# Another order for the first groups: chunks 4 and 5 ahead of weights, scores ahead of state products, q of the first chunks scaled by VectorE

## The chip, the cores and the metric

The kernel runs on one NeuronCore of a Trainium2 chip. A core has five instruction queues that run at the same time and wait for each other by semaphores: TensorE (PE in the profile; its weight loads are PEld), VectorE (DVE), ScalarE (ACT), GpSimd (POOL) and SyncE (SP, which here only issues DMA transfers). Each of them takes its instructions strictly in the order in which the program wrote them. Time is device microseconds (us) from start to end of an execution; lower is better.

## The reference

Two stages. The first is linear attention with a decay per head, over 4 batches, 8 heads, 768 positions and 64 features per head, in blocks of 64 positions. The second takes the result as 3072 tokens of 512 features through a two-layer network with a leaky ReLU.

```
for b in range(nb):                       # blocks of 64 positions
    intra = einsum('bhic,bhjc->bhij', qb, kb) * Dmask
    intra = einsum('bhij,bhjd->bhid', intra, vb)
    inter = einsum('bhid,bhde->bhie', qb * lam_pow, kv_state)
    out[:, :, sl] = intra + inter
    kv_state = lam_block * kv_state + einsum('bhsd,bhse->bhde', kb * rev_pow, vb)
x = out.transpose(0, 2, 1, 3).reshape(3072, 512)
h = x @ w_in                              # 512 x 2048, float64 input
return maximum(0.01 * h, h) @ w_out       # 2048 x 512, float64 input
```

## The kernel before, in words

**Tiling.** The tokens are cut into 24 chunks of 128 (two blocks of 64 each; 6 chunks per batch), and chunks are gathered into 6 groups of 4 (`GC = 4`, 512 tokens). The hidden width of 2048 is cut into 8 weights of 256 columns (`NP`), called p. Both products of the network are computed in split form: each operand is held as a high part h, a low part l and a mixed part m (`xh`, `xl`, `xm` for the tokens, `wh`, `wl`, `wm` for weights), and a product is three matmul passes, h by h, l by l and m by m.

**A chunk of attention** goes through these steps.
- `load_kq`, `load_v` (L335, L374): SP issues the loads of k, q (two transfers of 128 KB each) and v (one of 256 KB). The tiles exist twice, by the chunk's parity.
- `transposes` (L389): TensorE turns k and q round. k goes to the PSUM bank named by `KT` (b11) for the first four chunks and to `po` later, q goes to `pt`. ScalarE copies both out (L400, L401).
- L405 scales k in place by a decay, on GpSimd, or for chunks below `KM` on GpSimd or VectorE, whichever the planner sees free first. L409 scales q: for chunks below `QS` VectorE does it straight from `pt`, for others GpSimd from the copy.
- `scores` (L310, writes `psc`): 64 small matmuls in two halves. `go` makes the scores, `kv` makes the state products. Then VectorE masks the scores (L435) and adds the state products to the state (L440 or L442), once for each of the two blocks; between them GpSimd decays the state (L445). `psc` exists once, so the scores of a chunk wait for the last state add of the chunk before.
- `outputs` (L310, writes `po`): `own` and the two halves of `inter`. Then ScalarE makes `xh` (L490), VectorE `xl` (L491) and `xm` (L493; its rank is raised by `LATER` in the first group).

**A weight of w_in** (`w_in`, `to_float32`, `parts`): ScalarE issues two loads of 512 KB (L549); the float64 words are turned into float32 by three ScalarE operations (L561, L563, L565) and two of VectorE (L567, L568) for each half; then come `wh` (L574 on ScalarE or L576 on VectorE), `wl` (L579) and `wm` (L585) on VectorE.

**An up product** `("up", g, p, lo, hi)`: group g by weight p, over chunks lo to hi of the group (all four when they are not given). It is two blocks of 128 hidden columns, each three products of four matmuls (L623) with 512 columns when it is whole; ScalarE scales between the passes (L641) and applies the leaky ReLU (L644); SP writes the result G to DRAM (L647). The result tile `gs` exists twice. The blocks go through banks b10, b11 and b2 in turn; the first `EARLY` blocks leave b11 out.

**Order.** Nothing of this order is found at run time. `seq` lists the steps: `("a", c)` a whole chunk, `("b", c)` loads and transposes of chunks c and c+1 and the scores of c, `("r", c)` a round (outputs of c, scores of c+1, loads and transposes of c+2), `("wi", p)` a weight, `("up", ...)`. A step's place in `seq` is the rank of its operations. `Plan.emit` then schedules all operations in a model of the five queues: it always takes the operation that can start earliest, and among equal ones that of lower rank. The model has a duration for each operation and a delay after it (`LAG`, 3.5 us for a DMA). In the first two groups (the part of `seq` that is written out by hand) a load is taken at its length; later it has a slack of 4 us. While the plan sees TensorE idle early on, it inserts filler transposes into b10 (`busy`, L263), until the first operation that needs b10.

Of the kernel before, what the change touches and what calls it, by code (L numbers as in the profile page):

```python
# [31 lines left out]
def _bc(ap, idx, n):  # L32
    a = [list(x) for x in ap.ap]
    return bass.AP(ap.tensor, ap.offset, a[:idx] + [[0, n]] + a[idx:])


class Plan:
# [23 lines left out]
    def add(self, eng, us, fn, reads=(), writes=(), rank=0.0):  # L61

        n, deps = len(self.ops), set()
        for k in reads:
            w, r = self.last.setdefault(k, [None, []])
            if w is not None:
                deps.add(w)
            r.append(n)
        for k in writes:
            w, r = self.last.setdefault(k, [None, []])  # L70
            if w is not None:
                deps.add(w)
            deps.update(r)
            self.last[k] = [n, []]
        deps.discard(n)
        ways = {eng: us} if isinstance(eng, str) else dict(zip(eng, us))
        if self.slack:
            self.more[n] = self.slack
        if self.chain is not None:
            self.chains[self.chain].append(n)  # L80
        self.ops.append((ways, fn, deps, (self.rank + rank, n), set(writes)))
# [81 lines left out]
def kernel(  # L163
# [21 lines left out]
    NG = NCH // GC  # L185
    T = GC * C
    WARM = 9
    LATER = 4.0
    KT, EARLY = "b11", 1
    QS = 0  # L190
    KM = 1
    NRAW = 3
    TURN = 3
    SLACK, GSLACK = 4.0, 2.0
    SUBL, FIRST = 0.75, -8.0

    DV = 12
# [12 lines left out]
    def ps(shape, name):  # L210
        return psum.tile(shape, F32, name=name, tag=name)
# [3 lines left out]
    psc = ps([P, 2, 2 * HP, C2], "psc")  # L215
# [51 lines left out]
    plan = Plan()  # L267
    plan.idle, plan.spare, plan.warm = busy, "b10", 1.3 + 0.22 * WARM
    add = plan.add
    steady = False  # L270

    def length(us, issue=0.5):

        return issue if steady else us

    def move(us, fn, reads, writes, issue=0.5, rank=0.0, slack=SLACK):

        plan.slack = slack if steady else 0.0
        if steady and not rank:
            rank = FIRST  # L280
        add("DMA", length(us, issue), fn, reads, writes, rank=rank)
        plan.slack = 0.0
# [26 lines left out]
    def quad(dst, rows, lhsT, rhs, cols, start=False):  # L309
        nc.tensor.matmul(dst[HALF[cols]], lhsT=lhsT[HALF[rows]], rhs=rhs[HALF[rows]], start=start, stop=True,  # L310
                         skip_group_check=True)

    def tokens(t):
        return slice(t * C2, (t + 1) * C2)
# [8 lines left out]
    def of(c):  # L323
        return c // NCB, c % NCB, c % 2
# [3 lines left out]
    def load_kq(c):  # L328
        b, n, i = of(c)
        for src, x, nm in ((k, 0, "k"), (q, 1, "q")):  # L330
            y, dst = src[b, :, n * C:(n + 1) * C, :], kqv[x][i]

            def go(y=y, dst=dst):
                for z in range(2):
                    nc.sync.dma_start(out=dst[:, z * HP:(z + 1) * HP, :], in_=y[z::2].rearrange("h p d -> p h d"))  # L335
            if nm == "k" or c < DV:
                move(1.15, go, [], [f"{nm}{i}"], issue=1.0)
# [13 lines left out]
    def load_subs(c):  # L351
        b, n, i = of(c)
        for nm, src, pieces in zip("kq", (k, q), subs(c)):
            for sub, lo, hi, keys in pieces:
                add("DVE", 0.0, lambda: None, [], keys)
                for y in range(lo, hi):
                    for a in range(4):
                        h = y // 2 + (2 * y + a // 2) % HP * 2
                        z = src[b, h, n * C:(n + TURN) * C, a % 2 * C4:(a % 2 + 1) * C4]
                        o = sub[a * C4:(a + 1) * C4, y - lo, :]  # L360
                        move(0.55, lambda o=o, z=z: nc.sync.dma_start(
                                out=o.rearrange("j (m i) -> j m i", i=C4), in_=z.rearrange("(m j) i -> j m i", j=C4)),
                            keys, [f"{nm}s{y}{a}"], issue=SUBL, rank=4.0 + (0.4 if steady else 0.2) * (4 * y + a))
# [8 lines left out]
    def load_v(c):  # L372
        b, n, i = of(c)
        move(1.15, lambda: nc.sync.dma_start(out=kqv[2][i], in_=v[b, :, n * C:(n + 1) * C, :].rearrange("h p d -> p h d")),  # L374
            [], [f"v{i}"])

    def transposes(c):
# [17 lines left out]
        def copies():  # L395
# [3 lines left out]
            if c < DV:  # L399
# [3 lines left out]
            nr = slice(0, C2 if n == NCB - 1 else P)  # L403
            add(*((("DVE", "POOL"), (0.7, 1.1)) if c < KM else ("POOL", 1.1)),
                lambda e="POOL": ENG[e].tensor_tensor(kr[nr], kr[nr], _bc(pow_k, 3, D)[nr], op=ALU.mult), ["fk"], [f"k{i}"])  # L405
            m = slice(1 if n == 0 else 0, 2)
            o, x = (z.rearrange("p y (t i) -> p y t i", t=2)[:, :, m, :] for z in (qsTs[i], pt if c < QS else qTs[i]))
            eng, e, us, dep = ("DVE", nc.vector, 0.7, "pt") if c < QS else ("POOL", nc.gpsimd, 1.2, f"qT{i}")
            add(eng, us, lambda: e.tensor_tensor(o, x, _bc(pow_q, 2, 2)[:, :, m, :], op=ALU.mult), ["fq", dep], [f"qsT{i}"])  # L409
# [3 lines left out]
    def scores(c):  # L413
        b, n, i = of(c)
        tk, tv, kT, qT = kqv[0][i], kqv[2][i], kTs[i], qTs[i]
        n_pu = 1 if n == NCB - 1 else 2

        def go():
            for y in range(HP):
                for t in range(2):  # L420
                    for x in range(2):
                        quad(psc[:, x, y, :], x, kT[:, y, tokens(t)], qT[:, y, tokens(t)], t, start=y == 0)

        def kv():
            for y in range(HP):
                for x in range(2):
                    for t in range(n_pu):
                        h = y // 2 + (2 * y + x) % HP * 2
                        quad(pu[t][:, y, :], t, tk[:, 2 * y + x, :], tv[:, h, :], x, start=y == 0)

        add("PE", 0.47, kv, [f"k{i}", f"v{i}"], ["psc"])
        add("PE", 0.47, go, [f"kT{i}", f"qT{i}"], ["psc"])

        def uses():
            add("DVE", 0.69, lambda: nc.vector.tensor_tensor(sc, psc[:, :, lower, :], decay, op=ALU.mult), ["psc", "fk"], ["sc"])  # L435
            for t in range(n_pu):
                j = 2 * c + t
                new = state[j % 4]
                if n == 0 and t == 0:
                    add("DVE", 0.42, lambda new=new: nc.vector.tensor_copy(new, pu[0]), ["psc"], [f"st{j % 4}"])  # L440
                else:
                    add("DVE", 0.42, lambda new=new, t=t: nc.vector.tensor_tensor(new, new, pu[t], op=ALU.add),  # L442
                        ["psc"], [f"st{j % 4}"])
                if n_pu == 2:
                    add("POOL", 0.7, lambda new=new, j=j: nc.gpsimd.tensor_tensor(state[(j + 1) % 4], new, _bc(lam_c, 2, D), op=ALU.mult),  # L445
                        [f"st{j % 4}", "fq"], [f"st{(j + 1) % 4}"])

        return uses

    def outputs(c, between=lambda: None):  # L450
# [38 lines left out]
        def uses():  # L489
# [3 lines left out]
            add("DVE", 0.7, lambda: nc.vector.scalar_tensor_tensor(xm, xl.bitcast(F32), -S, xh.bitcast(F32), op0=ALU.mult, op1=ALU.add),  # L493
                [h, l], [m], rank=LATER if c < GC else 0.0)

        return uses

    def alone(c):
        load_kq(c)
        load_v(c)  # L500
        transposes(c)()
        scores(c)()
        outputs(c)()

    def begun(c):

        for x in (c, c + 1):
            load_kq(x)
            load_v(x)
            transposes(x)()  # L510
        scores(c)()
# [158 lines left out]
    def down(g, p):  # L670

        nonlocal n_t
        for tb in range(GC):
# [43 lines left out]

    seq = [("a", 0), ("a", 1), ("a", 2), ("a", 3), ("wi", 1), ("b", 4), ("wi", 0), ("up", 0, 1), ("up", 0, 0), ("wi", 2),  # L720
           ("r", 4), ("wi", 3), ("up", 0, 2), ("up", 0, 3), ("r", 5), ("r", 6), ("r", 7), ("wi", 7), ("up", 1, 3, 0, 1),
           ("wi", 4), ("up", 1, 1, 0, 2), ("wi", 6), ("up", 0, 7), ("up", 0, 4), ("up", 1, 7, 1, 3), ("up", 0, 6),
           ("wi", 5), ("up", 0, 5), ("up", 1, 5), ("r", 8), ("r", 9), ("r", 10), ("up", 1, 7, 3, 4), ("r", 11),
           ("up", 1, 2), ("up", 1, 0), ("up", 1, 7, 0, 1), ("up", 1, 3, 1, 4), ("up", 1, 1, 2, 4), ("up", 1, 6),
           ("up", 1, 4)]
    nxt, n_out, begin = 3 * GC, 0, len(seq)
    steps = [(g, p) for g in range(2, NG) for p in range(NP)]
    for n, (g, p) in enumerate(steps):
# [17 lines left out]
    for n, x in enumerate(seq):  # L746
        plan.rank = float(n)
        steady = begin <= n and x[0] in ("r", "up", "wo")
# [50 lines left out]
```

## Time and profile before

| what | value |
|---|---|
| median of 3 runs | 617.78 us (616.84 to 617.81) |
| profiled execution | 617.28 us |
| its span (first to last instruction) | 615.4 us |
| PE busy | 604.8 us, 98% |
| DVE busy | 306.9 us, 50% |
| ACT busy | 270.7 us, 44% |
| POOL busy | 90.6 us, 15% |
| DMA moved | 104.67 MB, 170 GB/s |
| first up product (L623) starts at | 30.67 us |
| chunk outputs (first L310 to `po`) start at | 10.61, 15.02, 21.98, 28.28, 43.10, 52.68, 64.46, 73.53 us for chunks 0 to 7 |

Times within the span count from its start. A row of the timeline gives start, duration, engine, line, operation, the tile written and the tiles read, and in brackets how long the engine stood idle just before and what ended that. Matmuls are pipelined, so durations of consecutive matmul rows overlap; the distance between their starts is what one costs.

### The profile page before, as it was taken

To read this page: it belongs to the slowest core of one execution; us is meant where nothing else is said; L and a number is where in the kernel's file an instruction comes from. 1 tells how busy PE (TensorE), PEld (TensorE's weight loads), DVE (VectorE), ACT (ScalarE), POOL (GpSimd) and SP (SyncE) were. 2 spreads that over 40 slices of the span, in tenths; PEclk is the share of its full clock that TensorE was granted. 3 is DMA by queue.
4 is the path that set the end of the run, shared out by engine and by line. 5 is a ranking of instruction groups with operands and counts; after the bars stand their busy time and mean duration, and the time that the engine had idled before them with its cause. 6 is when DMAs were issued, how large, how long until landed. Compare 5 with 4: busy or idle time off the path is not lost.

```text
span 615.4 us, 13097 instructions
## 1 busy us (share of the span) xinstructions
PE 604.8 (98%) x5482; PEld 503.8 (82%) x5482; DVE 306.9 (50%) x409; ACT 270.7 (44%) x436; POOL 90.6 (15%) x95
## 2 busy tenths in 40 slices
PE   8799999999999999999999999999999999999997
PEld 7588988898888888888788888888888888888885
DVE  4799883520353324315356755635454554636431
ACT  3688884434465645656577622221222313214111
POOL 4862522420332114104000000000000000000000
PEclk9999999999999999999999999999999999999999
DMA  9999866656657978886686862523433343433201
GB/s 197 236 262 268 236 193 161 159 146 141 180 166 225 239 212 223 220 239 191 240 281 228 268 179 80 194 69 112 163 100 128 115 136 104 136 103 124 82 1 69
DMA packets 142235, 104.67 MB, mean 170 GB/s; under 512 B 117088, under 2 KB 119136, under 8 KB 142176
## 3 DMA queue, kind: packets, MB, share of 16 engines
q1 hardware_dynamic: 137680, 95.44, 53.2%
q10 hardware_dynamic: 4496, 8.39, 4.4%
q8 instruction: 43, 0.70, 0.5%
q14 instruction: 16, 0.13, 0.1%
HBM read 68.16 MB, written 35.65 MB: 169 GB/s over the span
## 4 chain that ended last, share of the span: by engine, by line
PE 96%; DMA 2%; POOL 0%; SPq 0%; DVE 0%; issue 0%; ACT 0%; DVEq 0%
PE b L623 44%; PE b L682 18%; PE po L682 11%; PE psc L682 11%; PE po L310 4%; PE pt L682 4%; PE psc L310 4%; DMA att<-in_q_dram 2%; PE pt L389 1%; PE po L389 1%; PE b L263 1%; DMA att<-in_k_dram 1%; PE b L389 0%; SPq L335 0%; POOL att L405 0%
## 5 line engine op out<-in xcount | busy, mean ns | idle before, releaser
L664 ACT ACTIVATE xh<-att 128x1024 fp32r<-128x1024 f32 x48 | 50.9, 1061 | 145.9 <-PE po L682 144.0
L665 DVE SCALAR_TENSOR_TENSOR xl<-att,xh 128x1024 fp32r<-128x1024 f32 x48 | 58.7, 1222 | 97.0 <-ACT xh L664 97.0
L623 PE MATMUL b<-xh,wh 128*128 128x512 f32 (+3 forms) x416 | 105.8, 377 | 0.0
L623 PE MATMUL b<-xl,wl 128*128 128x512 f32 (+3 forms) x416 | 105.5, 377 | 0.0
L623 PE MATMUL b<-xm,wm 128*128 128x512 f32 (+3 forms) x416 | 104.8, 381 | 0.0
L623 PEld LDWEIGHTS b<-xl,wl 128*128 128x128 f32 x416 | 75.3, 188 | 14.5 <-DVE wl L579 0.2
L623 PEld LDWEIGHTS b<-xh,wh 128*128 128x128 f32 x416 | 75.0, 188 | 14.8 <-ACT gs L644 0.7
L623 PEld LDWEIGHTS b<-xm,wm 128*128 128x128 f32 x416 | 73.6, 188 | 14.5 <-ACT b L641 0.4
L641 ACT ACTIVATE b<-b 128x512 f32<-128x512 f32 (+2 forms) x98 | 56.3, 576 | 56.2 <-PE b L623 55.8
L644 ACT ACTIVATE gs<-b 128x512 f32<-128x512 f32 (+2 forms) x98 | 57.2, 587 | 43.5 <-PE b L623 39.9
L682 PE MATMUL b<-wh,xh 128*128 128x512 f32 x192 | 74.7, 389 | 0.0
L682 PE MATMUL b<-wl,xl 128*128 128x512 f32 x192 | 74.7, 389 | 0.0
L667 DVE SCALAR_TENSOR_TENSOR xm<-xl,xh 128x1024 fp32r<-128x1024 f32 x48 | 58.8, 1226 | 5.1 <-DVE xl L665 0.5
L435 DVE TENSOR_TENSOR att<-psc,att 128x512 f32<-128x512 f32 x24 | 16.5, 689 | 73.7 <-PE psc L310 73.5
L409 POOL TENSOR_TENSOR att<-att 128x512 f32<-128x512 f32 (+1 forms) x24 | 29.0, 1209 | 95.9 <-PE po L310 66.8
L682 PEld LDWEIGHTS b<-wl,xl 128*128 128x128 f32 x192 | 36.1, 188 | 7.6
L682 PEld LDWEIGHTS b<-wh,xh 128*128 128x128 f32 x192 | 36.0, 187 | 7.5
L405 POOL TENSOR_TENSOR att<-att 128x512 f32<-128x512 f32 (+1 forms) x24 | 28.4, 1182 | 73.0 <-PE po L389 34.2
L445 POOL TENSOR_TENSOR att<-att 128x256 f32<-128x256 f32 x40 | 33.4, 836 | 30.9 <-DVE att L442 25.6
L682 PE MATMUL po<-wm,xm 128*128 128x512 f32 (+1 forms) x100 | 37.2, 381 | 0.7 <-ACT raw L704 0.7
L682 PE MATMUL psc<-wh,xh 128*128 128x512 f32 x96 | 37.4, 389 | 0.0
L682 PE MATMUL psc<-wl,xl 128*128 128x512 f32 x96 | 37.3, 389 | 0.0
(71 smaller groups left out, 799.4 us busy)
## 6 DMA issues: line engine op xcount, KB each, us to landing
att<-g SPq DMA_DIRECT2D x48, 512.0 KB, 3.3
g<-gs SPq DMA_DIRECT2D x45, 512.0 KB, 3.7
raw<-in_moe_w_in_dram ACTq DMA_DIRECT2D x16, 512.0 KB, 5.0
raw<-in_moe_w_out_dram SPq DMA_DIRECT2D x16, 512.0 KB, 4.7
att<-in_k_dram SPq DMA_DIRECT2D x48, 128.0 KB, 4.5
att<-in_v_dram SPq DMA_DIRECT2D x24, 256.0 KB, 4.7
out_dram<-gs SPq DMA_DIRECT2D x23, 256.0 KB, 2.0
wo<-w SPq DMA_DIRECT2D x8, 512.0 KB, 5.8
```

The source lines that it names most:

```text
L310: nc.tensor.matmul(dst[HALF[cols]], lhsT=lhsT[HALF[rows]], rhs=rhs[HALF[rows]], start=start, stop=True, skip_group_check=True)
L405: lambda e="POOL": ENG[e].tensor_tensor(kr[nr], kr[nr], _bc(pow_k, 3, D)[nr], op=ALU.mult), ["fk"], [f"k{i}"])
L409: add(eng, us, lambda: e.tensor_tensor(o, x, _bc(pow_q, 2, 2)[:, :, m, :], op=ALU.mult), ["fq", dep], [f"qsT{i}"])
L435: add("DVE", 0.69, lambda: nc.vector.tensor_tensor(sc, psc[:, :, lower, :], decay, op=ALU.mult), ["psc", "fk"], ["sc"])
L445: add("POOL", 0.7, lambda new=new, j=j: nc.gpsimd.tensor_tensor(state[(j + 1) % 4], new, _bc(lam_c, 2, D), op=ALU.mult), [f"st{j % 4}", "f ...
L623: nc.tensor.matmul(dst, lhsT=w[z][:, kk * 2 * P + f * P:kk * 2 * P + (f + 1) * P], rhs=x[z][:, kk, toks], start=start and kk == 0, stop=kk ...
L641: add("ACT", ns, lambda b=b: nc.scalar.activation(out=b, in_=b, func=AF.Copy, bias=0.0, scale=S + 1.0), [], [kb], rank=-1.5)
L644: add("ACT", ns, lambda b=b, r=r: nc.scalar.activation(out=r, in_=b, func=AF.Prelu, bias=0.0, scale=1.0 / WS, alpha=0.01), [kb], [f"gs{jg} ...
L664: add("ACT", 1.05, lambda: nc.scalar.activation(out=h, in_=graw[j], func=AF.Copy, bias=0.0, scale=NEAR), reads, wr("h"))
L665: add("DVE", 1.25, lambda: nc.vector.scalar_tensor_tensor(l, graw[j], 1.0, h.bitcast(F32), op0=ALU.mult, op1=ALU.subtract), reads + [f"rh{ ...
L667: add("DVE", 1.25, lambda: nc.vector.scalar_tensor_tensor(m, l.bitcast(F32), -S, h.bitcast(F32), op0=ALU.mult, op1=ALU.add), [f"rh{j}", f" ...
L682: nc.tensor.matmul(acc[tb][z // 2][:, cols], lhsT=ring[j][z][:, f * T + tb * P:f * T + (tb + 1) * P], rhs=W[pp][z][:, f * d_model:(f + 1) ...
```

## The change

Chunks 4 and 5: in the written-out order, the rounds of chunks 4 and 5 move ahead of the weights 0, 2 and 3, and the up products of group 0 follow their weights less tightly. In group 1, weights 3 and 7 are no longer cut into pieces; weight 1 stays in two pieces of two chunks. For chunks 0, 1 and 2 `go` is issued ahead of `kv` (`GOFIRST = 3`). `QS = 4` makes VectorE scale q of chunks 0 to 3 from `pt`; `KM = 2` lets VectorE also take k of chunk 1. `EARLY = 0` lets the first up blocks use all three banks in turn. `LATER` is 2 in place of 4. In the hand-written part the plan takes every DMA to land 1 us later than before (`EARLY_SLACK = 1.0`, before 0). The computation is the same.

```diff
-    LATER = 4.0
-    KT, EARLY = "b11", 1
-    QS = 0
-    KM = 1
+    LATER = 2.0
+    KT, EARLY = "b11", 0
+    QS = 4
+    KM = 2
...
+    EARLY_SLACK = 1.0
+    GOFIRST = 3
...
-        plan.slack = slack if steady else 0.0
+        plan.slack = slack if steady else EARLY_SLACK
...
+        if c < GOFIRST:
+            add("PE", 0.47, go, [f"kT{i}", f"qT{i}"], ["psc"])
         add("PE", 0.47, kv, [f"k{i}", f"v{i}"], ["psc"])
-        add("PE", 0.47, go, [f"kT{i}", f"qT{i}"], ["psc"])
+        if c >= GOFIRST:
+            add("PE", 0.47, go, [f"kT{i}", f"qT{i}"], ["psc"])
...
-    seq = [("a", 0), ("a", 1), ("a", 2), ("a", 3), ("wi", 1), ("b", 4), ("wi", 0), ("up", 0, 1), ("up", 0, 0), ("wi", 2),
-           ("r", 4), ("wi", 3), ("up", 0, 2), ("up", 0, 3), ("r", 5), ("r", 6), ("r", 7), ("wi", 7), ("up", 1, 3, 0, 1),
-           ("wi", 4), ("up", 1, 1, 0, 2), ("wi", 6), ("up", 0, 7), ("up", 0, 4), ("up", 1, 7, 1, 3), ("up", 0, 6),
-           ("wi", 5), ("up", 0, 5), ("up", 1, 5), ("r", 8), ("r", 9), ("r", 10), ("up", 1, 7, 3, 4), ("r", 11),
-           ("up", 1, 2), ("up", 1, 0), ("up", 1, 7, 0, 1), ("up", 1, 3, 1, 4), ("up", 1, 1, 2, 4), ("up", 1, 6),
-           ("up", 1, 4)]
+    seq = [("a", 0), ("a", 1), ("a", 2), ("a", 3), ("wi", 1), ("b", 4), ("r", 4), ("up", 0, 1), ("wi", 0), ("r", 5),
+           ("wi", 2), ("wi", 3), ("up", 0, 0), ("up", 0, 2), ("r", 6), ("up", 0, 3), ("up", 1, 1, 0, 2), ("wi", 7),
+           ("wi", 6), ("up", 0, 7), ("r", 7), ("wi", 5), ("up", 1, 7), ("wi", 4), ("up", 1, 2), ("up", 0, 6),
+           ("up", 0, 5), ("up", 0, 4), ("up", 1, 0), ("up", 1, 6), ("up", 1, 1, 2, 4), ("r", 8), ("up", 1, 5),
+           ("r", 9), ("r", 10), ("up", 1, 3), ("r", 11), ("up", 1, 4)]
```

## The prediction

> **What bounds the kernel now.** I read the page first, then the stages (busy time by window), then the chain of work in order of time for the first 110 us, then the timeline of the first 65 us and of the stretch from 128 to 165 us.
>
> ```profile
> PE 604.8 (98%) x5482; PEld 503.8 (82%) x5482; DVE 306.9 (50%) x409; ACT 270.7 (44%) x436; POOL 90.6 (15%) x95
> ...
> PE 96%; DMA 2%; POOL 0%; SPq 0%; DVE 0%; issue 0%; ACT 0%; DVEq 0%
> ```
>
> TensorE sets the end: 98% busy, 96% of the chain. So a change can win in two ways only: fewer microseconds of TensorE work, or fewer in which TensorE has nothing useful. Of the latter nearly all lie ahead of the first up product (L623, xh by wh), at 30.67 us. Four chunks of attention cost TensorE about 3.0 us each (8 transposes 0.88, scores 1.05, outputs 1.1), 12 us, and q of chunks 4 and 5 0.9: about 13 of these 30.67 us are work, the rest is waiting or the L263 filler (8.4 us busy).
>
> ```profile
> 20.00:30.00 10.00, 7.51 (x215) 5.70 (x216) 7.33 (x12) 6.35 (x12) 7.31 (x7) 1.00 0.94 231
> 30.00:40.00 10.00, 10.00 (x110) 8.33 (x111) 9.33 (x12) 8.86 (x16) 6.41 (x5) 1.00 1.04 277
> 40.00:50.00 10.00, 10.00 (x152) 8.33 (x151) 9.47 (x12) 8.63 (x16) 3.90 (x4) 1.00 0.86 255
> 50.00:60.00 10.00, 10.00 (x170) 8.58 (x169) 9.37 (x13) 8.86 (x17) 2.57 (x2) 1.00 0.86 256
> ```
>
> The columns are window, length, busy time of PE, its weight load, DVE, ACT and POOL, granted clock, DMA share and GB/s. From 30 us on TensorE is full. But VectorE stands at 93 to 95%, ScalarE at 86 to 89% and DMA near its limit: in this stage the three that prepare the weights have almost no room either.
>
> ```profile
> 14.33 0.84 SPq L335
> ...
> 15.22 5.92 DMA att<-in_q_dram
> ...
> 23.08 4.79 DMA att<-in_q_dram
> 27.91 0.44 PE pt L389 x2
> 28.35 0.86 PE po L310 x48
> ```
>
> This is the chain. Two loads of q are on it, 10.7 us together. The first is q of chunk 3, the second q of chunk 5, and the last two rows show why the second counts: the transposes of chunk 5, which is not yet needed, stand ahead of chunk 3's outputs (po) in TensorE's order.
>
> ```profile
> 20.23 0.41 DVE L442 TENSOR_TENSOR att<-att,psc 128x256 f32<-128x256 f32 x1
> ...
> 22.37 1.28 POOL L409 TENSOR_TENSOR att<-att 128x512 f32<-128x512 f32 x1 [1.57 <-ACT att L401]
> ...
> 23.61 0.81 POOL L445 TENSOR_TENSOR att<-att 128x256 f32<-128x256 f32 x1
> ...
> 24.92 1.02 PEld L310 LDWEIGHTS psc<-att 64*64 64x64 f32 x64 [0.48 <-DVE att L442]
> ```
>
> A second, parallel hold. The state of chunk 2 was added at 20.64 (L442), but its decay (L445, POOL) began at 23.61: POOL stood at L409, scaling q of chunk 3, which waited for that q. Only after that decay and one more add could chunk 3's scores start, at 24.92.
>
> **The change part by part.**
>
> *Fewer pieces of up products.* Before, group 1 has weight 3 in pieces of 1+3 chunks and weight 7 in 1+2+1; after, both are whole, and only weight 1 stays 2+2. The price from starts of consecutive products of four matmuls:
>
> ```profile
> 128.21 0.61 PE L623 MATMUL b<-xh,wh 128*128 128x128 f32 x4
> 128.66 0.61 PE L623 MATMUL b<-xl,wl 128*128 128x128 f32 x4
> ...
> 132.87 0.85 PE L623 MATMUL b<-xl,wl 128*128 128x384 f32 x4
> 133.57 0.64 PE L623 MATMUL b<-xh,wh 128*128 128x256 f32 x4
> 134.04 0.64 PE L623 MATMUL b<-xl,wl 128*128 128x256 f32 x4
> ...
> 141.73 1.07 PE L623 MATMUL b<-xh,wh 128*128 128x512 f32 x4
> 142.63 1.07 PE L623 MATMUL b<-xl,wl 128*128 128x512 f32 x4
> ```
>
> So 0.45 us for 128 columns, 0.70 for 384, 0.47 for 256, 0.90 to 0.91 for 512. An up has six such products. Weight 3: 6 x (0.45 + 0.70 - 0.91) = 1.4. Weight 7: 6 x (0.45 + 0.47 + 0.45 - 0.91) = 2.8. Together **-4.2 us** of TensorE work, all on the path, since TensorE is full where these pieces ran. [...]
>
> *q scaled by VectorE for chunks 0 to 3 (QS 4).* Removes L409 four times from POOL (0.72 + 3 x 1.28 us). Chunk 2's decay can then follow POOL's L405 of chunk 3, which ended at 20.81, instead of 23.61. Decay 0.8, add 0.4, hand-overs 0.3: psc is free at about 22.3; q of chunk 3 is copied by 22.29 (its landing at 21.14, transposes, L401). Scores then start at 22.4, and outputs at 24.6 (1.1 scores, 0.7 for L435, 0.4 of hand-overs), against 28.28. On VectorE it adds four reads of pt, priced by L435, also a PSUM source: 0.69, and 0.41 for the half-width first one, 2.5 us in all. VectorE has 3 of each 10 us free there, so most is hidden; uncovered, the one of chunk 3 stands ahead of chunk 2's last state add: 0 to +0.7, taken as **+0.3**. pt is also held until VectorE has read it.
>
> *Loads assumed 1 us later (EARLY_SLACK).* The planner's idea of a q load was 1.15 + 3.5 = 4.65 us; the chain shows 5.92 and 4.79. With 1 us more it should no longer place chunk 5's transposes ahead of chunk 3's outputs. Only both parts together give 28.28 - 24.6 = **-3.7 us** at the first product (30.67 to about 27.0). Bounds: 0, where chunk 5's transposes stay in front; -5, where q of chunk 3 itself comes earlier. First-product weight parts are there: wh of weight 1 ended at 26.57, wl at 28.31, wm at 30.38 against a need of about 27.0, 28.8, 30.6.
>
> *Scores ahead of state products in chunks 0 to 2 (GOFIRST).* Half of the 1.16 us pair moves: L435 starts 0.55 earlier, and the state products end as before. Against it, k of chunk 3 on SP waits for chunk 1's state products, and q of chunk 3 is behind it on that queue (14.33): up to +0.5. In favour, 3 x 0.55 if the loads were not the gate. I take 0.
>
> *Chunks 4 and 5 ahead of weights.* Round 4 is ranked ahead of weight 0, round 5 ahead of weights 2 and 3. So VectorE does up to 2.9 us (L435 0.69, two L442 0.83, L491 and L493 1.4) and ScalarE 1.9 us per chunk before the weights. On SP, k, q and v of chunks 6 and 7 (2, 2 and 1 issues each, of 128 or 256 KB) go ahead of the first G writes; k of 6 waits for chunk 4's state products, and a G write behind it holds a gs buffer, of which there are two. Weight loads are issued by ScalarE and share the same full DMA. What covers it: from 27.0 TensorE has the first up (5.4), chunk 4 (2.2 left), scores of 5 (1.1) and eight to sixteen transposes (0.9 to 1.8), to about 37. wh of weight 0 ended at 37.7 in the old trace; with 2.9 us of VectorE ahead of it and the 2.7 us free from 20 to 30 partly used, 37.7 to 40.6. That gives back 0 to 3.4: **+1.8**, the middle. Further weights follow at the same spacing as before, since the work is the same, and later there is more ready work per weight.
>
> *The rest* (LATER, KM, bank order by EARLY 0): choices of engine, rank or bank for single operations of 0.7 to 1.1 us, in stages where their engine or bank is free by the trace (b11 last read at 20.35). 0, or 0.5 each way.
>
> Sum on the span: -4.2 - 3.7 + 0.3 + 1.8 = -5.8, so 615.4 becomes 609.6. The profiled execution took 617.28, 1.9 beyond its span: 611.5. The median of the runs shown is 617.78, 0.5 above it: **612.0**.
>
> **The rivals.**
> *Pieces only.* The start gain is nil, either because chunk 5's transposes still stand in front or because the weights come no sooner and TensorE waits for them instead: 617.8 - 4.2 = 613.6. For it: VectorE at 93 to 95%. Against: VectorE and ScalarE idle 27 and 36% from 20 to 30 us.
> *Starved, slower.* Weights 0, 2, 3 (and 7) come late because chunks 4 and 5 take VectorE first, and the whole-width products of group 1 that replace the small pieces can't run until chunk 7 is through. 3 us at each of four weights is 12, less 4.2 and less the 3.5 of the start, plus a price that no row here shows: the longest wait of TensorE past 3 us is 1.1. [...] Together +6: 623.8; it decides from 4.2 + 3.5 = 7.7 us of new waits on. In its favour: the small pieces of 59 and 66 us ran just when the old order needed ready work. Against: the 2-chunk piece of weight 1 is placed right there.
> *All of it.* q of chunk 3 comes earlier and weights keep up: -4.2 - 5: 608.5.
>
> **How the numbers follow.** Forecast 50%, own range 610 to 614; pieces only 18%; starved 20%, with half of it under 620 since waits of 8 us are likelier than 14; all of it 12%. The range is 607 to 619: it leaves out the upper part of the starved case and a little below. This kernel's measurement can tell about 0.2%, 1.2 us. Faster: the first, second and fourth case less 8 in 100 that fall short by extra waits, 72%. Same 7%, slower 21%.
>
> **What would show it.** Right: no 128- or 384-column L623 products; first L623 near 27 us; no L409 of 128x512 on POOL before 25 us; chunk 3's po outputs ahead of chunk 5's pt transposes; TensorE full from there. Wrong: TensorE waits on wh, wl or wm (L576, L579, L585) between 30 and 70 us, the first L623 still near 30 us, or a cold clock past 10 us.

## The result and the profile after

The changed kernel takes 614.11 us (median of 5 runs, 613.74 to 614.32) against 617.03 us (616.54 to 617.81): ratio 0.995, 95% interval 0.9935 to 0.9964. That is 2.9 us faster. The forecast was 612.0 with a range of 607 to 619, so the direction and the range hold, but only half of the forecast gain of 5.8 us came. The line numbers after are 2 to 5 higher than before (L623 is now L628, L682 is L687, L435 is L440, L409 is L411).

The page of the changed kernel, busy times, the chain's shares and the up products:

```profile
span 612.5 us, 12915 instructions
...
PE 600.0 (98%) x5402; PEld 497.8 (81%) x5402; DVE 312.4 (51%) x412; ACT 270.8 (44%) x434; POOL 82.7 (14%) x90
...
PE 93%; DVE 4%; DMA 1%; POOL 1%; issue 0%; ACT 0%; SPq 0%; DVEq 0%; ACTq 0%; POOLq 0%
...
L628 PE MATMUL b<-xh,wh 128*128 128x512 f32 (+1 forms) x392 | 102.7, 386 | 0.8 <-ACT xh L495 0.8
```

TensorE works 4.8 us less than before (600.0 against 604.8), and of the up products only one other form is left (256 columns, 16 of each kind; before there were 128, 256 and 384). But the span fell by 2.9 us only. VectorE has 4% of the chain here (0% before); in a second profile of the same kernel it again has 0%, so this share says little.

The first 50 us of the changed kernel by stage (columns as before: window, length, PE, weight load, DVE, ACT, POOL, clock, DMA share, GB/s):

```profile
20.00:30.00 10.00, 8.25 (x268) 6.74 (x272) 8.81 (x16) 6.56 (x12) 6.23 (x6) 1.00 1.12 256
30.00:40.00 10.00, 8.72 (x114) 6.88 (x115) 9.76 (x13) 7.08 (x13) 5.70 (x5) 1.00 1.00 269
40.00:50.00 10.00, 9.39 (x149) 7.68 (x147) 9.28 (x12) 8.05 (x16) 5.10 (x4) 1.00 0.79 219
50.00:60.00 10.00, 10.00 (x166) 8.50 (x167) 9.62 (x15) 9.08 (x17) 4.08 (x3) 1.00 0.83 238
```

Before, TensorE was full from 30 us on. Now it lacks 1.9 us between 30 and 50 (0.8 us in the second profile). The timeline of TensorE names the places: the first up product, a transpose behind it and the second pass of weight 2.

```profile
31.16 2.14 PE L628 MATMUL b<-xh,wh 128*128 128x512 f32 x8 [0.78 <-ACT xh L495]
...
33.79 0.66 PE L391 MATMUL po<-att 128*128 128x128 f32 x4 [0.49 <-DVE xl L496]
...
49.94 1.20 PE L628 MATMUL b<-xl,wl 128*128 128x512 f32 x4 [0.61 <-DVE wl L584]
```

The first up product starts at 31.16 us, 0.5 later than before, not 3.7 earlier. It waits there for `xh` of the last chunk (L495), not for a weight.

**Where the 2.9 us are.** Four points of the two traces divide the span: the first up product (L623 or L628), the first down product (L682 or L687, from its weight load), the last matmul (from its weight load) and the end.

| stretch | before, us | after, us | difference |
|---|---|---|---|
| start to first up product | 30.67 | 31.16 | +0.5 |
| first up to first down product | 317.3 | 314.0 | -3.3 |
| down products | 263.3 | 263.0 | -0.3 |
| last matmul to the end | 4.1 | 4.3 | +0.2 |

In the second stretch TensorE is busy for 317.0 us before and 312.7 after, so its work fell by 4.3; its idle time there rose from 0.3 to 1.4 us.

### The profile page after: what moved, and what is told of

The parts are those of the page before. It is cut to its first block, busy times and chain, and to the rows that moved or that the text cites. A ratio compares the mean times of both kernels' runs of the same rounds, so it can differ in the third digit from the quotient of the medians.

```text
span 612.5 us, 12915 instructions
## 1 busy us (share of the span) xinstructions
PE 600.0 (98%) x5402; PEld 497.8 (81%) x5402; DVE 312.4 (51%) x412; ACT 270.8 (44%) x434; POOL 82.7 (14%) x90
## 3 DMA queue, kind: packets, MB, share of 16 engines
q10 hardware_dynamic: 4496, 8.39, 4.4%
## 4 chain that ended last, share of the span: by engine, by line
PE 93%; DVE 4%; DMA 1%; POOL 1%; issue 0%; ACT 0%; SPq 0%; DVEq 0%; ACTq 0%; POOLq 0%
PE b L628 41%; PE b L687 18%; PE po L687 11%; PE psc L687 11%; PE po L312 4%; PE pt L687 4%; PE psc L312 3%; DVE w L572 1%; DVE w L573 1%; DMA att<-in_v_dram 1%; PE pt L391 1%; DVE wm L590 0%; DVE att L447 0%; DVE wl L584 0%; DVE wh L581 0%
## 5 line engine op out<-in xcount | busy, mean ns | idle before, releaser
L628 PE MATMUL b<-xh,wh 128*128 128x512 f32 (+1 forms) x392 | 102.7, 386 | 0.8 <-ACT xh L495 0.8
L628 PE MATMUL b<-xl,wl 128*128 128x512 f32 (+1 forms) x392 | 102.9, 387 | 0.6 <-DVE wl L584 0.6
L628 PE MATMUL b<-xm,wm 128*128 128x512 f32 (+1 forms) x392 | 103.2, 391 | 0.0
L628 PEld LDWEIGHTS b<-xh,wh 128*128 128x128 f32 x392 | 72.7, 188 | 16.0 <-ACT xh L495 0.9
L628 PEld LDWEIGHTS b<-xl,wl 128*128 128x128 f32 x392 | 72.5, 188 | 15.7 <-DVE wl L584 1.0
L628 PEld LDWEIGHTS b<-xm,wm 128*128 128x128 f32 x392 | 71.3, 188 | 14.6
L646 ACT ACTIVATE b<-b 128x512 f32<-128x512 f32 x96 | 56.0, 585 | 50.7 <-PE b L628 50.6
L649 ACT ACTIVATE gs<-b 128x512 f32<-128x512 f32 x96 | 57.2, 597 | 47.4 <-PE b L628 43.8
L687 PE MATMUL b<-wl,xl 128*128 128x512 f32 x192 | 74.8, 390 | 0.0
L687 PE MATMUL b<-wh,xh 128*128 128x512 f32 x192 | 74.8, 390 | 0.0
L440 DVE TENSOR_TENSOR att<-psc,att 128x512 f32<-128x512 f32 x24 | 16.5, 690 | 65.6 <-PE psc L312 65.5
L687 PEld LDWEIGHTS b<-wh,xh 128*128 128x128 f32 x192 | 36.1, 188 | 7.6 <-ACT gs L649 0.2
L687 PEld LDWEIGHTS b<-wl,xl 128*128 128x128 f32 x192 | 36.1, 188 | 7.4
L407 POOL TENSOR_TENSOR att<-att 128x512 f32<-128x512 f32 (+1 forms) x23 | 25.6, 1111 | 100.5 <-PE po L391 55.2
L687 PE MATMUL po<-wm,xm 128*128 128x512 f32 (+1 forms) x100 | 37.2, 382 | 0.7 <-ACT raw L709 0.7
L572 DVE TENSOR_SCALAR w<-w 128x512 int32<-128x512 int32 x32 | 17.7, 553 | 39.0 <-ACT w L566 38.9
L687 PE MATMUL pt<-wm,xm 128*128 128x512 f32 x96 | 37.4, 390 | 0.0
L687 PE MATMUL po<-wl,xl 128*128 128x512 f32 x96 | 37.4, 390 | 0.0
```

What stands on the lines that cost most here:

```text
L572: add("DVE", 0.42, lambda: nc.vector.tensor_scalar(d, d, 3, None, op0=ALU.logical_shift_left), [], [key])
L628: nc.tensor.matmul(dst, lhsT=w[z][:, kk * 2 * P + f * P:kk * 2 * P + (f + 1) * P], rhs=x[z][:, kk, toks], start=start and kk == 0, stop=kk ...
L646: add("ACT", ns, lambda b=b: nc.scalar.activation(out=b, in_=b, func=AF.Copy, bias=0.0, scale=S + 1.0), [], [kb], rank=-1.5)
L649: add("ACT", ns, lambda b=b, r=r: nc.scalar.activation(out=r, in_=b, func=AF.Prelu, bias=0.0, scale=1.0 / WS, alpha=0.01), [kb], [f"gs{jg} ...
L687: nc.tensor.matmul(acc[tb][z // 2][:, cols], lhsT=ring[j][z][:, f * T + tb * P:f * T + (tb + 1) * P], rhs=W[pp][z][:, f * d_model:(f + 1) ...
```

## The experiments

Four theories stood against each other at first. A: the whole gain is TensorE work that whole products of weights 3 and 7 save; the new constants lose a part of it at the front (all that lies ahead of the first up product). B: the gain is in the order of chunks and weights. C: it is in the constants (q on VectorE above all). The other letters ask about single pieces of the front. The table gathers all runs; "first up" and "first down" are starts in the profiled execution, the ratio is to the kernel before on the same chip. The front alone differs by about 1 us from profile to profile: the same first instructions led to 31.16, 31.45 and 30.30 (the changed kernel twice, and with the cuts put back).

| run | median, us | ratio (95%) | first up | first down |
|---|---|---|---|---|
| before, its own profile | 617.03 | 1 | 30.67 | 348.0 |
| after, its own profile | 614.11 | 0.995 (0.9935 to 0.9964) | 31.16 | 345.2 |
| order list only | 617.46 | 1.000 (0.9982 to 1.0019) | 30.61 | 347.1 |
| before, whole products | 614.99 | 0.9958 (0.9941 to 0.9976) | 30.55 | 345.8 |
| after, cut again | 619.74 | 1.0032 (1.0014 to 1.0049) | 30.30 | 348.9 |
| constants only | 619.88 | 1.0031 (1.0015 to 1.0047) | 30.32 | 349.9 |
| after, GOFIRST 0 | 615.42 | 0.9972 (0.9953 to 0.9992) | 30.47 | 345.3 |
| after, QS 0 | 619.67 | 1.0032 (1.0011 to 1.0054) | 32.42 | 348.2 |
| after, EARLY_SLACK 0 | 616.98 | 0.9993 (0.9976 to 1.001) | 30.95 | 348.8 |
| after, weight loads later | 627.0 | 1.0163 (1.0133 to 1.0192) | 30.8 | 356.7 |
| after, state add first | 614.26 | 0.9968 (0.9952 to 0.9983) | 29.10 | 343.9 |
| after, mask on scores alone | 620.68 | 1.0061 (1.0041 to 1.0081) | 32.11 | 348.5 |
| the last two together | 616.58 | 0.9993 (0.9977 to 1.0009) | 32.14 | 346.2 |
| after, once more | 614.56 | 0.9967 (0.9955 to 0.9978) | 31.45 | 344.9 |

**The order list alone.** The kernel before with the new `seq`, constants untouched.

```diff
-    seq = [("a", 0), ... ("b", 4), ("wi", 0), ("up", 0, 1), ...
+    seq = [("a", 0), ... ("b", 4), ("r", 4), ("up", 0, 1), ("wi", 0), ("r", 5), ...
```

> The new order list alone, with all constants of the kernel before. Theory A (the gain is the 4.2 us of TensorE work that whole products of weights 3 and 7 save, and the new constants lose a part of it at the front): 617.0 - 4.2 = 612.8, first up product at 30.7 us as before, less than 1 us of new waits of TensorE. Theory B (the gain is in the order of chunks and weights): between 612 and 614.5, too. Theory C (the gain is in the constants, q on VectorE above all): 616.5 to 617.5.

Measured: no gain at all. TensorE is busy 600.9 us, so the work did fall, but new waits took it back. The largest is the first product of weight 0. VectorE's and TensorE's rows of this run:

```profile
38.77 0.42 DVE L442 TENSOR_TENSOR att<-att,psc 128x256 f32<-128x256 f32 x1 [0.52 <-POOL att L445]
39.11 0.69 DVE L576 TENSOR_SCALAR wh<-w 128x1024 fp32r<-128x1024 f32 x1
...
39.85 1.21 PE L623 MATMUL b<-xh,wh 128*128 128x512 f32 x4 [1.27 <-DVE wh L576]
```

`wh` of weight 0 stands behind both state adds of chunk 4 (L442), the second of which waits for GpSimd. In the changed kernel the new constants put it ahead of that chunk's mask, from 37.47 us:

```profile
37.47 1.44 DVE L581 TENSOR_SCALAR wh<-w 128x1024 fp32r<-128x1024 f32 x1
...
38.83 0.68 DVE L440 TENSOR_TENSOR att<-psc,att 128x512 f32<-128x512 f32 x1
```

So chunk 4 ahead of weight 0 costs TensorE 1.3 us of waiting in this run, and none of it where the new constants move `wh` forward again. A had expected less than 1 us of waits here, and 612.8; it missed by 4.7 us.

**Whole products alone.** The kernel before, where the pieces of weights 3 and 7 are dropped and each is taken whole at the place of its last piece. Up to the first up product TensorE's order is that of the kernel before.

```diff
-("up", 1, 3, 0, 1), ... ("up", 1, 7, 1, 3), ... ("up", 1, 7, 3, 4), ... ("up", 1, 7, 0, 1), ("up", 1, 3, 1, 4),
+("up", 1, 7), ("up", 1, 3),
```

> The order before, where weights 3 and 7 in group 1 are taken whole at the place of their last piece; constants and everything else as before. A: 612.8, TensorE stays full after the first up product. B: 616 to 617.5, because TensorE waits between 55 and 85 us where the pieces were taken away. C: as B.

Measured: 614.99, that is 2.3 us under the 617.28 of its chip, between A and B. From first up to first down product it takes 315.2 us, 2.1 less than before; 4.2 were on offer. TensorE's idle time in that stretch rose from 0.3 to 1.6 us; the rest of the difference was not traced. B had looked for waits between 55 and 85 us: TensorE is full from 50 to 80, and the longest new wait comes only behind that:

```profile
82.43 0.46 PE L310 MATMUL po<-att 64*64 64x64 f32 x16 [0.88 <-ACT att L474]
```

This run says most about the change. With the old order and the old constants, whole products alone reach 0.9958 (0.9941 to 0.9976); the changed kernel has 0.995 and 0.9967. These can't be told apart: nothing that was measured needs more than the whole products.

**The pieces again.** The changed kernel with the cuts put back, side by side at the place of the whole products.

```diff
-("up", 1, 7), ... ("up", 1, 3),
+("up", 1, 7, 0, 1), ("up", 1, 7, 1, 3), ("up", 1, 7, 3, 4), ... ("up", 1, 3, 0, 1), ("up", 1, 3, 1, 4),
```

> The changed kernel with weights 3 and 7 in group 1 cut again into 1+3 and 1+2+1, side by side at the place of the whole ones. It prices the pieces alone. A: 614.1 + 4.2 = 618.3. [...] B: 614 to 615.

Measured: 1.0032. Against 0.995 and 0.9967 for the changed kernel this is 0.65 to 0.82%, 4.0 to 5.1 us; the stretch from first up to first down product grows from 314.0 to 318.6, by 4.6. TensorE's busy time in that stretch grows by 4.5 us (317.2 against 312.7). The worked-out 4.2 stands.

**The constants alone.** The new constants with the old `seq`.

```diff
-    LATER = 4.0
-    KT, EARLY = "b11", 1
-    QS = 0
-    KM = 1
+    LATER = 2.0
+    KT, EARLY = "b11", 0
+    QS = 4
+    KM = 2
...
+    EARLY_SLACK = 1.0
+    GOFIRST = 3
```

> The new constants (QS, KM, EARLY, LATER, EARLY_SLACK, GOFIRST) with the order list before. A: 617.0 + 0.5 to 1.5 = 617.5 to 618.5, first up product at 31 us or later. B: 616.5 to 617.5. C: 613.5 to 615, first up product before 30 us.

Measured: 1.9 us slower than before, with the first up product at 30.32. A's direction was right, its place was not: the loss comes after the first up product, which starts no later. Two of its new waits:

```profile
45.84 0.46 PE L312 MATMUL po<-att 64*64 64x64 f32 x16 [0.51 <-DVE att L479]
...
61.29 1.21 PE L628 MATMUL b<-xm,wm 128*128 128x512 f32 x4 [0.76 <-ACT b L646]
```

Neither half of the change is worth anything alone (0 and +1.9 us by their ratios), and together they give -2.9. The order list holds the whole products too, and there their gain was lost to new waits. So A is right about where the gain comes from, and not about the rest: whether this work shows in the time depends on the waits around it, and these do not add up part by part.

**Scores first, undone.**

```diff
-    GOFIRST = 3
+    GOFIRST = 0
```

> The changed kernel with GOFIRST 0: state products ahead of scores in chunks 0 to 2 again. In the changed kernel's profile the mask of chunk 0 (L440) began at 11.12 us, only when the state products, too, had ended (11.05), and three fillers stand between the two halves. Theory D (scores first gains nothing, and the split pair costs the front about 1 us): first up product at 30 us or before, 613 to 614. Theory E (scores first helps): the masks of chunks 0 to 2 end 0.5 us later each, 615 to 616.

Measured: 0.9972, on its chip; the changed kernel has 0.995 and 0.9967, and the intervals overlap. First down product 345.3 against 345.2 and 344.9. Its 615.42 lies in E's range, but on a chip where the kernel before took 0.7 us more than beside the changed kernel. Scores first is worth nothing that these runs can tell, and costs nothing either: neither D nor E is shown.

**q back on GpSimd.**

```diff
-    QS = 4
+    QS = 0
```

> The changed kernel with QS 0: q of chunks 0 to 3 scaled by GpSimd from the copy again. Theory F (VectorE's scaling freed GpSimd and brought chunk 3's scores 2.5 us nearer to chunk 2's): first up product 1.5 to 3 us later, at 33 us, 615.5 to 617. Theory G (L411 waits for ScalarE's copy anyway and stands ahead of the state add in VectorE's order, so nothing is won): first up product at 30 to 31.5 us, 613.5 to 614.5.

Measured: 1.0032, 4 to 5 us slower than the changed kernel. F had the direction, not the size: the first up product comes at 32.42, which explains 1 us, and the order of everything behind it changed with it. A load of k is waited for at a new place, for instance:

```profile
65.87 0.44 PE L391 MATMUL po<-att 128*128 128x128 f32 x2 [1.24 <-DMA att<-in_k_dram]
```

**No slack for early loads.**

```diff
-    EARLY_SLACK = 1.0
+    EARLY_SLACK = 0.0
```

> The changed kernel with EARLY_SLACK 0: every early load planned 1 us sooner. The first weight load then stands behind ScalarE's copy of chunk 0's q. Theory H (the slack puts that load ahead of the copy, where it waits for an earlier load to land, and delays the front by 1 to 3 us): first up product before 30 us, 611.5 to 613. Theory I (the slack keeps transposes that wait for q out of TensorE's way, as the prediction had it): transposes of q wait over 2 us for loads, first up product after 31.5 us, 615 to 617.

Measured: 616.98. It fell between the theories: H was right that ScalarE's copy of chunk 0's q comes sooner (6.52 in place of 7.38 us), chunk 0's mask too (8.39 in place of 11.12), and wrong that this wins anything. TensorE's first up product in the timeline, and the stage it is in (the columns of the stages, with the clock third from the end):

```profile
30.95 3.78 PE L628 MATMUL b<-xh,wh 128*128 128x512 f32 x8 [2.66 <-ACT xh L495]
```

```profile
30.00:40.00 10.00, 9.05 (x92) 7.36 (x93) 4.75 (x8) 6.45 (x11) 3.88 (x4) 0.70 0.75 201
```

After 2.7 us of waiting, eight matmuls take 3.78 us in place of 2.14, at 0.43 us each where the changed kernel took 0.23: about half the rate. The trace's clock record stands at 0.50 from 29.17 to 36.00 us. TensorE worked through the last 5 us of that, so some 2.5 us are lost to the clock (an estimate: half of 5).

**Weight loads behind the first copy.** The first three loads of w_in are planned only after L403 of chunk 0.

```diff
-            to_float32("wi", p, h, w32[:, h, :], f"w32{h}")
+            to_float32("wi", p, h, w32[:, h, :], f"w32{h}", ["qT0"] if n_raw < NRAW else ())
```

> The changed kernel where the first three weight loads are planned only after chunk 0's copy of q (L403). Theory H: the copy of chunk 0's q starts at 6.6 us in place of 7.4, chunk 1's scores before 15 us, first up product 0.5 to 1.5 us sooner unless the weight itself comes late; 613 to 614. If it is the weight that comes late: TensorE waits on wh (L579 or L581) before the first up product, 615 to 617.

Measured: 1.6% slower, worse than either line expected. The copy does start at 6.61 us, but all three loads move far back, and the first up product at 30.8 shows no use of it. Later TensorE waits up to 5 us for a load of k and runs at a granted clock of 0.83 to 0.94 between 40 and 70 us. It is too blunt to price the one load. (No slack, above, had the copy early as well, at 6.52 us, and its first up product was no earlier either.)

**State add ahead of the scaling of q.** The plan is told that L411 needs ScalarE's copy, which it waits for anyway (below).

```diff
-            add(eng, us, ..., ["fq", dep], [f"qsT{i}"])
+            add(eng, us, ..., ["fq", dep, f"qT{i}"], [f"qsT{i}"])
```

> The changed kernel where the plan is told that VectorE's scaling of q (L411) also needs ScalarE's copy, as it does in fact. In the changed kernel L411 of chunk 1 waited for that copy until 14.65 us and stood ahead of the state add (L447), whose decay had ended at 13.82; now the state add stands ahead. Theory J (this place costs the front about 1.4 us): chunk 1's scores at 14.5 us in place of 15.8, first up product 0.5 to 1.5 us sooner (29.7 to 30.7), 612.5 to 613.5. Rival K (loads, not the chain of states, set the front after chunk 1): first up product within 0.5 us of 31.2, 613.5 to 614.5.

Measured: the place is as J said. VectorE's rows for chunk 1 in this run show the state add first, and the scores at once after it:

```profile
12.14 0.42 DVE L447 TENSOR_TENSOR att<-att,psc 128x256 f32<-128x256 f32 x1 [1.26 <-POOL att L450]
...
12.78 0.69 DVE L411 TENSOR_TENSOR att<-pt,att 128x512 f32<-128x512 f32 x1 [0.21 <-ACT att L403]
12.80 1.02 PEld L312 LDWEIGHTS psc<-att 64*64 64x64 f32 x64 [0.43 <-ACT att L403]
```

Chunk 1's mask starts at 14.03, against 15.14 in the unchanged kernel on the same chip, so this place is worth 1.1 us there. The first up product starts at 29.10 against 31.45. Not all of these 2.35 us belong to the edit: the unchanged one also waited for v of chunk 3 and then ran at half clock for 3.4 us (in the part on the prediction, below). And the time does not follow: 614.26 against 614.56, ratios 0.9968 and 0.9967. Of the 2.35 us, 1.3 are given back by the first down product (343.9 against 344.9), and the profiled spans end 1.05 apart (611.2 and 612.2), which the medians don't confirm. Two new waits for weights are among what gives it back:

```profile
46.16 2.11 PE L628 MATMUL b<-xh,wh 128*128 128x512 f32 x8 [0.28 <-ACT wh L579]
...
55.46 2.14 PE L628 MATMUL b<-xh,wh 128*128 128x512 f32 x8 [0.28 <-ACT wh L579]
```

They are not all of it. TensorE's idle time between the two points is 0.8 us in both runs, so most of the 1.3 us lies in a longer busy time, which was not traced.

**The mask on the scores alone**, and **both edits**.

```diff
-            add("PE", 0.47, go, [f"kT{i}", f"qT{i}"], ["psc"])
+            add("PE", 0.47, go, [f"kT{i}", f"qT{i}"], ["psc", "pscg"])
...
-            add("DVE", 0.69, ..., ["psc", "fk"], ["sc"])
+            add("DVE", 0.69, ..., ["pscg", "fk"], ["sc"])
```

> The changed kernel where the plan is told that the mask (L440) needs only the scores, not the state products. If scores first can pay at all, the mask of chunk 0 starts while the state products run, 0.5 to 1.3 us sooner than 11.1 us, and the time is 613 to 614. If the mask still waits until both have ended, the times of the front stay as in the changed kernel within 0.5 us, and so does the total, 613.5 to 615.

> Both edits together, the copy ahead of L411 and the mask on the scores alone. J: 612 to 613.5, first up product at 29.5 to 30.5 us. K: 613.5 to 615.

Measured: 1.0061 and 0.9993, both slower than any line expected; the first up product comes at 32.1 in both. TensorE's second half and the mask of chunk 0, with the first edit alone:

```profile
9.95 1.13 PE L312 MATMUL psc<-att 64*64 64x64 f32 x32
11.15 0.69 DVE L440 TENSOR_TENSOR att<-psc,att 128x512 f32<-128x512 f32 x1 [2.69 <-PE psc L312]
```

The mask still starts only when the state products have ended (11.08), though its own half had ended at 9.2. VectorE waits there for a semaphore of TensorE (109 in the trace), and no matmul of the first half raises it; the first that does starts at 10.34, in the second half. So the program gives the mask no earlier signal, although it reads only the half of `psc` that the scores write; why, was not found. The plan moved other work for a start that does not come; that this is what made the kernel slower is likely, but not shown.

**The changed kernel once more.**

> The changed kernel itself, once more, on the chip of the three others: ratio to the kernel before 0.994 to 0.9965, first up product at 30.2 to 31.2 us, as the front of the changed kernel differed by 0.9 us between two runs of the same instructions up to there (31.16, and 30.29 with the pieces cut again).

Measured: 0.9967, at the edge of what was expected; its first up product, 31.45, came 0.25 later than expected. No version tried is measurably faster than the changed kernel.

## Why the prediction was right, and where it was not

**Fewer pieces, -4.2: right.** The cuts put back cost 4.0 to 5.1 us, and whole products alone gave 2.3 us without the rest of the change. The distance of starts was the right price: 111 ns for a 128-column matmul before (eight in 0.89 us, from 128.21 to 129.10). Each of these matmuls has a weight load of its own (5482 of each before), and 256 columns cost hardly more than 128 (0.47 against 0.45 us for four). What sets this distance was not shown.

**First product 3.7 us earlier: this step failed.** It came 0.5 us later, and in the second profile 0.8 later; no run here has it near 27 us. Chunk 3's scores were to start at 22.4 us; they start at 25.5 in both profiles, against 24.92 before. Starts of the mask (L435 before, L440 after) mark how far the chain of chunks is:

| | chunk 0 | 1 | 2 | 3 | first up |
|---|---|---|---|---|---|
| before | 9.84 | 14.03 | 19.63 | 26.16 | 30.67 |
| after | 11.12 | 17.04 | 21.68 | 27.73 | 31.16 |
| after, once more | 9.84 | 15.14 | 19.90 | 26.98 | 31.45 |
| gap to the one before, change | +1.3 | +1.7 | -1.0 | -0.5 | -1.1 |
| the same, once more | 0 | +1.1 | -0.8 | +0.5 | 0 |

Only two of these changes stand in both profiles: chunk 1 is reached later, and chunk 2 sooner after it. One thing that the prediction named came true: chunk 5's transposes of q no longer stand ahead of chunk 3's outputs, at least of their first 48 matmuls.

```profile
28.47 0.93 PE L312 MATMUL po<-att 64*64 64x64 f32 x48
29.33 0.66 PE L391 MATMUL pt<-att 128*128 128x128 f32 x4
```

*Chunk 1, shown by a run.* What the prediction had not seen is VectorE's order in the changed kernel:

```profile
13.20 0.62 POOL L450 TENSOR_TENSOR att<-att 128x256 f32<-128x256 f32 x1
...
14.65 0.69 DVE L411 TENSOR_TENSOR att<-pt,att 128x512 f32<-128x512 f32 x1 [2.51 <-ACT att L403]
...
15.26 0.41 DVE L447 TENSOR_TENSOR att<-att,psc 128x256 f32<-128x256 f32 x1
```

The decay ended at 13.82, but the state add came at 15.26, behind the new L411, which waited for ScalarE to finish copying the same `pt`. In the kernel before, the same add followed its decay (11.67 to 12.29) at once:

```profile
12.32 0.42 DVE L442 TENSOR_TENSOR att<-att,psc 128x256 f32<-128x256 f32 x1 [1.47 <-POOL att L445]
```

The prediction had priced q on VectorE by its 0.69 us of work (+0.3) and had looked at chunk 3; the cost was the wait that the new instruction carries, 1.4 us (1.3 in the second profile), and it fell at chunk 1. With the state add ahead, chunk 1's mask is back at 14.03, so this place causes that gap.

*Chunk 0, traced.* With loads planned 1 us later, the first weight load (issued by ScalarE) slipped ahead of ScalarE's copy of chunk 0's q, which starts at 7.38 in place of 6.61. The prediction had checked what SP issues, but not what ScalarE issues. The copy and the scores before, then the chain of the changed kernel in order of time (start, duration, what):

```profile
6.61 0.59 ACT L401 COPY att<-pt 128x512 f32<-128x512 f32 x1 [0.69 <-PE pt L389]
...
7.78 1.99 PE L310 MATMUL psc<-att 64*64 64x64 f32 x64
```

```profile
2.88 4.05 DMA att<-in_v_dram
...
6.96 0.38 ACTq L554
...
7.38 0.59 ACT att L403
...
8.02 1.13 PE psc L312 x32
9.16 0.83 PE b L265 x3
9.99 1.06 PE psc L312 x32
```

The load waits until v of chunk 0 has landed: the trace shows the program's DMAs on eight semaphores in turn (100 to 103, 105 to 108), and this load waits for 106, the one of v. The scores start only 0.2 us later for it, but their two halves now have three fillers (L265) between them, and the mask waits for both halves:

```profile
11.12 0.69 DVE L440 TENSOR_TENSOR att<-psc,att 128x512 f32<-128x512 f32 x1 [2.69 <-PE psc L312]
```

This is not what holds the first up product. In the second profile the copy is as late (7.34) and the fillers are there, but the mask starts at 9.84, because the same matmuls ran faster:

```profile
7.98 0.69 PE L312 MATMUL psc<-att 64*64 64x64 f32 x32 [1.47 <-ACT att L403]
```

The trace's clock record shows the full clock from 5.75 us on in this profile, from 12.84 in the first one and from 10.19 in the kernel before, and nothing ahead of that. So an early clock, which the change does not set (the same kernel has 12.84 and 5.75), goes with matmuls fast enough to make up for the order here, and the first up product was late all the same. The run without slack, with the copy at 6.52 and the mask at 8.39, had it at 30.95.

*Chunk 3, traced but not tested.* In the second profile TensorE waits there for v of chunk 3, and then the granted clock is half from 26.23 to 29.65 us:

```profile
25.51 1.43 PE L312 MATMUL psc<-att 64*64 64x64 f32 x64 [1.85 <-DMA att<-in_v_dram]
```

```profile
20.00:30.00 10.00, 7.96 (x199) 6.44 (x198) 7.78 (x12) 5.49 (x11) 5.22 (x5) 0.83 1.08 254
```

TensorE was nearly always busy in these 3.4 us, so they cost about 1.7 us (an estimate: half of them). Without them its first up product would have come at about 29.8, still far from 27.

**Weights late, +1.8: right in kind, too large.** From first up to first down product 0.9 of the 4.2 us is missing, 0.3 in the second profile. The run with the state add ahead hints that the term grows with an earlier start: it gave back 1.3 of 2.35 us. Had the front come 3.7 us earlier, much of that might not have reached the end. The sum took the two terms as independent, and they may not be.

**Scores first, 0:** right, no difference that the run could tell.

The sum as measured, on the span: -4.2 (pieces), +0.5 (front), +0.9 (waits after it), -0.1 (end), together -2.9, where -4.2 - 3.7 + 0.3 + 1.8 = -5.8 was forecast. One term carried the gain, and it was right by its reason. The front was wrong by 4.2 us, as much as the whole gain from the pieces; that the time stayed in the range owes something to its width and to late weights that cost less than allowed for. The size is that of the rival "pieces only" (613.6), but neither of its two reasons for a nil start was the one: chunk 5's transposes no longer stood in front, and the first product waited for `xh`, not for a weight. In the sum of the slower rival, 1.7 of the +6 (6 less 12 - 4.2 - 3.5) is a price that no run shows. What the runs showed in its place are two stretches with the clock record at 0.50, of 6.8 and 3.4 us, around waits of 2.7 and 1.85 us, neither of them for a weight; by the estimates above they cost about 2.5 and 1.7 us.

What stays open: why the new order needs the new constants as a whole. One wait of 1.3 us (weight 0 in the order-list run) was shown; the rest of the 4.8 us that part the sum of the two halves from the whole was not traced. Nor is it shown that order and constants together add anything to the whole products.

## What to carry to other kernels

An instruction moved to another engine brings its waits along: look at what it will wait for and at what then stands behind it in that engine's order, before pricing its duration. When a bound engine loses work, the gain shows only as far as new waits do not eat it: of 4.2 us saved alone, only 2.3 showed, and with the new order list alone none did. When a change has many parts, try the smallest part that removes work by itself: here it did as well as the whole. Profile the same kernel twice before reading a front of 30 us to half a microsecond. And price a cut into pieces by the distance of starts in the trace, not by its columns alone.

## What the runs showed of the hardware

- TensorE's clock was halved around short waits in two profiles. In the run without slack the clock record goes to 0.50 at 29.17 us, 0.9 us into a wait of 2.7, and stays there for 6.8 us (0.43 us a matmul in place of 0.23). In the second profile of the changed kernel it does so at 26.23, after a wait of 1.85 us, for 3.4 us.
- The same 64 small matmuls of chunk 0 took 1.13 us a half or 0.69 us a half in different executions. The first clock record came at 12.84 us in the slow one and at 5.75 us in the fast one; the profile's rows print 1.00 for the time ahead of it, when nothing is recorded.
- VectorE's read of `pt` began only when ScalarE's copy of the same tile had ended, for chunks 0 to 2 (8.00 after 7.97, 14.65 after 14.62, 18.22 after 18.18 us), although both only read it; the profile puts each of these starts down to that copy.
